# Turning tables and activation rows on TensorE instead of in DMAs, in a fused spectral filter and squared-ReLU kernel

## The chip, the core and the metric

The kernel runs on one core of a Trainium2 chip. The core has TensorE (PE, matrix products into PSUM), VectorE (DVE), ScalarE (ACT), GpSimd (POOL), SyncE (SP, which here issues every DMA) and 16 DMA engines. The metric is the device time of one execution in microseconds (us). All engines take their own instructions in order and wait for each other on semaphores.

## The reference

One token matrix of 2048 x 512 in bf16 goes through a spectral filter and then through a feed-forward layer (FFN), each behind a layer norm and each with a residual:

```python
def _A_ref(x, w_r, w_i):
    X = rfft2(x.astype(float32), axes=(-2, -1))
    X = X * (w_r + 1j * w_i)
    return irfft2(X, s=(S, D), axes=(-2, -1)).astype(bfloat16)

def _B_ref(x, w1, b1, w2, b2):
    h = einsum("bsd,df->bsf", x, w1) + b1
    r = where(h > 0, h, 0)
    return einsum("bsf,fd->bsd", r * r, w2) + b2

h  = x + _A_ref(_layernorm(x), A_w_r, A_w_i)
h2 = h + _B_ref(_layernorm(h), B_w1, B_b1, B_w2, B_b2)
```

D is 512, the FFN's inner width F is 1792.

## The kernel before

The tokens are laid out as 128 partitions by G = 16 groups (`xs`, token 16p + g), all in SBUF for the whole run. The two-dimensional Fourier transform and its inverse are done as matrix products with tables of cosines and sines that the kernel makes itself by integer ramps and ScalarE's sine. There are four stretches.

**Opening (about 0 to 18 us).** Loads of x; layer-norm statistics; the tables `KF`, `GF` and `EF`; the first product `p1` with `KR` (KF times the reciprocal deviation) into `Bt`.

**Middle (about 18 to 49.5 us).** For each of eight frequency blocks pr: the product `p2` (16 matmuls of 256 columns, for a pair of halves), its cast `U` on ACT, the product `p3` with `EF` (4 matmuls of 512 columns, or 12 for blocks 5 to 7), its cast `AB` on ACT, a butterfly `X` on DVE (blocks 1 to 4), the product `m` with the filter on DVE, two combinations `Z` and two folds `M` on DVE, the inverse product `p4` with `EI` on PE, its cast `T2` on ACT. Names such as p4-3-0 mean product p4, block 3, first half. At the end comes a short head for the first two token groups: `pd` (a product with `GI`), its cast `EO`, `yt`, the square `sq`, the sum `ss`, a logarithm and an exponential, and the normalised transposed rows `UT0`; beside it `py`, which with b2 gives the residual `hb`.

**FFN (about 49.5 to 154 us).** The 16 groups go in five chunks (2, 3, 4, 4 and 3 groups). Each chunk has 14 up products (`ph`/`sg` banks, L952), ReLU on ACT (L964), square on DVE (L970), and then the down products (`po`, L981). Between those, the next chunk is made ready: `p5`, `od`, `q`, `R`, `p6`, `hs` = x plus the filter's output, sum of squares on ACT (L757), reciprocal deviation on POOL (L896 to L900), the normalised rows `u` (L906 or L908), and their turned form `UT`, which the next chunk's up products read.

The transposed tables are made by DMA: `EI` from `EF` and `CN`, `KI` from `KF`, `GI` from `GF` (L454 to L465). So are `UT` of the groups in `TURN` = 2 and 5 to 15 (L801 and L921); groups 3 and 4 are turned by four 128 x 128 PE products into a `pp` bank (L932), which ACT or DVE copies to SBUF (L937). `GI`'s odd rows get a factor per partition from POOL (L495).

What sets the order: `Plan` takes every task with an estimated duration, reads, writes, a priority and a buffer, and hands out the order of each engine by its own clock of estimates. For the middle the order of PE, ACT and DVE is instead written out by hand (`MID`, L760), as is the start of the FFN (`DRAIN`, L995). The order of POOL and SP is always the planner's. Buffers matter: in the middle the large PSUM tiles `mm` are three, `U`, `m`, `X`, `Z` and `M` have two buffers each, `AB` three. `Z` of block 0 is read by p4-0 and so holds one of the two Z buffers until p4-0 is done.

Four lines that the prediction comes back to:

```python
EI = fwd.tile([P, 4, 9, P], BF16, name="EI")                 # L211
pool(0.5, lambda e=e: gp.tensor_scalar(GI[:, 1 + 2 * e], GI[:, 1 + 2 * e], hrow[:], 1.0, ALU.mult, ALU.mult), 410.0,  # L495
TURN = (2, *range(5, G))                                      # L801
pe.transpose(p[:, P * d:P * d + P], T["u", c][:, i, bass.ts(d, P)], ident[:])   # L932
```

Of the kernel before, what the change touches and what calls it, by code (L numbers as in the profile page):

```python
# [9 lines left out]
ALU = mybir.AluOpType  # L10
# [23 lines left out]
class Plan:  # L34
# [13 lines left out]
    def add(self, eng, w, fn, reads=(), writes=(), prio=0.0, alloc=None, at=0.0, shared=False, lag=0.0,  # L48
            uses=(), order=(), name=None):
        many = isinstance(eng, tuple)  # L50
        ways = dict(zip(eng, w)) if many else {eng: w}
        t = dict(many=many, eng=None, ways=ways, w=0.0, fn=fn, reads=list(reads), writes=list(writes), prio=prio, alloc=alloc, at=at,
                 shared=shared, lag=lag, end=None, order=list(order), n=len(self.tasks),
                 name=name or "-".join(map(str, writes[-1] if isinstance(writes[-1], tuple) else writes[-1:])))
        self.tasks.append(t)
        for k in t["writes"]:
            self.made.setdefault(k, []).append(t)
        for k in set(t["reads"]) | set(t["writes"]) | set(uses):
            self.use.setdefault(k, []).append(t)
# [85 lines left out]
def kernel(  # L145
# [52 lines left out]
    sq0 = persist.tile([P, 2, ND, P], BF16, name="sq0")  # L198
    rsb = persist.tile([P, 2, P], FP32, name="rsb")
    UT0 = persist.tile([P, 2, ND, P], BF16, name="UT0")  # L200
    EO = persist.tile([P, 2, 2, 256], BF16, name="EO")
    junk = persist.tile([P, D], BF16, name="junk")
    fz = persist.tile([P, 512], BF16, name="fz")
# [64 lines left out]
    def flat(t):  # L268
        n = len(t.shape)
        return t if n == 2 else t.rearrange("p a b -> p (a b)") if n == 3 else t.rearrange("p a b c -> p (a b c)")  # L270
# [180 lines left out]
            add(eng, ((0.37, 0.59), (0.42, 0.67))[t][n - 1], e2, reads=[k] + ["Btw"] * t, order=[("va", 4)] * t,  # L451
                writes=["Bt"] + ["BtD"] * (t == 1 and b == G), prio=56 + a)

    def tr_dma(i, dst, src, dep, prio):  # L454
        add("SP", 2.5, lambda: sy.dma_start(dst, src, transpose=True), reads=dep, order=[("EI", 2)] * (i == 3) + [("Wr", 1)] * (i < 2), writes=[("EI", i)], prio=prio, lag=(10.6, 10.4, 6.0, 6.0)[i])
    for i in range(2):
        tr_dma(i, EI[:, i], flat(EF[:, i]), [f"EF{i}"], 12 + i)
    tr_dma(3, KI[:], flat(KF[:]), ["KF"], 16)
    tr_dma(2, EI[:, 2], flat(EF[:, 2]), ["EF2"], 15)
    for pr in BY_Z:  # L460
        add("SP", 1.2, lambda pr=pr: sy.dma_start(EI[:, 3, pr], CN[:, pr - PE0], transpose=True), reads=["CN"],
            order=[("EI", 3)], writes=[("EI", 3, pr)], prio=17, lag=6.0)
    for t in range(2):
        add("SP", 1.3, lambda t=t: sy.dma_start(GI[:, :, P * t:P * t + P], flat(GF[:, t]), transpose=True), reads=[("gf", t)],
            order=[("EI", 3)], writes=[("gi", t)], prio=40.5 + t / 10, lag=12.0)  # L465
    for k, (d, s) in ((0, (W1[:], B_w1.rearrange("(c p) f -> p c f", p=P))),
                      (1, (W2[:], B_w2.rearrange("(i p) d -> p i d", p=P))),
                      (3, (b2b[:], B_b2.unsqueeze(0).to_broadcast([P, D])))):
        add("SP", 0.7, lambda d=d, s=s: sy.dma_start(d, s), writes=[("FW", k)], prio=40 + k, lag=15.0,
            order=[("gi", 1)] * (k > 0) + [("EI", i) for i in range(4)] + [("Wr", 0), ("Wr", 1), ("Wn", 0), ("Wn", 1)])  # L470

    PE0 = 5
    BY_PE = tuple(range(PE0, 8))
# [7 lines left out]
    def mid_tasks():  # L481
        def b1t():
            p = sg_tile(("b1",))
            mm(p[:, 0:NF], lhsT=b1b[:], rhs=ident[0:NF, 0:NF], start=True, stop=True)
            for g in range(2):
                mm(p[0:2, P + P * g:2 * P + P * g], lhsT=nmh[:, g], rhs=ident[:], start=True, stop=True)
        act(0.19, lambda: sc.copy(nmt[:], T[("b1",)][0:2, P:3 * P].rearrange("p (g c) -> p g c", g=2)), 142.0, reads=[("b1",)],
            writes=["nmt"], name="nmt")
        add("PE", 0.2, b1t, reads=["b1b", "ident", "nmh"], order=[("p3", 3)], writes=[("b1",)], prio=141.0, alloc=("sg", ("b1",)))
        act(0.19, lambda: sc.copy(b1f[:], T[("b1",)][:, 0:NF]), 142.0, reads=[("b1",)], writes=["b1f"])  # L490
        act(1.4, lambda: sc.preload_act_table_set("natural_log_exp_and_others"), 0.0, reads=["eps"], writes=["sqrt"])

        pool(0.2, lambda: gp.memset(ones[:], 1.0), 400.0, writes=["ones"])
        for e in range(2):
            pool(0.5, lambda e=e: gp.tensor_scalar(GI[:, 1 + 2 * e], GI[:, 1 + 2 * e], hrow[:], 1.0, ALU.mult, ALU.mult), 410.0,  # L495
                 reads=["hv", ("gi", 0), ("gi", 1)], writes=["GI"], name=f"GI-{e}")
        pool(0.15, lambda: gp.tensor_copy(nmh[:, :, 0], nm1[:, 0:2]), 401.0, reads=["nm1"], writes=["nmh0"])
        pool(0.15, lambda: gp.tensor_tensor(nmh[:, :, 1], nm1[:, 0:2], nmh[:, :, 0], ALU.subtract), 402.0, reads=["nmh0"],
             writes=["nmh"])
# [218 lines left out]
        for d in range(ND):  # L718
            mm(T["yt", g][:, P * d:P * d + P], lhsT=xs[:, g, P * d:P * d + P], rhs=ident[:], start=False, stop=False)
    for g in range(2):  # L720
        add("PE", 0.22, lambda g=g: cen(g), reads=["ones", "nmt"], order=[("p3", 7)], writes=[("yt", g, 0)],
            uses=[("yt", g)], name=f"yt-{g}-0", prio=170.0, alloc=("sg", ("yt", g)))
        add("PE", 0.22, lambda g=g: res(g), reads=["ident"], order=[("yt", g, 0)], uses=[("yt", g)],
            writes=[("yt", g, 1)], name=f"yt-{g}-1", prio=170.0)

    for g in range(2):
# [23 lines left out]
        def ut0(g=g):  # L750
# [2 lines left out]
        dve(0.66, ut0, -30.0, reads=[("r2", 0, g)], uses=[("yt", g)],   # L753
            writes=[("UT", 0), "UT0b" if g else "UT0a"], name=f"UT0-{g}")

    def sq_of(src, g):
        sc.activation(junk[:], src, ACT.Square, bias=nm1[:, g:g + 1], accum_out=ss2[:, g:g + 1])  # L757

    T["UT", 0] = UT0
    MID = {  # L760
        "PE": "p3-1 p2-2-0 p2-2-1 p2-4-0 p2-4-1 p2-3-0 p3-2 p2-3-1 p3-4 p2-6-0 p2-6-1 p3-3 p4-0-0 b1 "
             "p4-0-1 p3-6 p2-5-0 p2-5-1 p2-7-0 p2-7-1 p4-2-0 p4-2-1 p4-1-0 p4-1-1 p3-5 p3-7 p4-3-0 "
             "p4-3-1 p4-4-0 p4-4-1 p4-6-0 yt-0-0 p4-6-1 p4-5-0 yt-0-1 p4-5-1 p4-7-0a p4-7-1a p4-7-0b "
             "pd-0 pd-1 yt-1-0 yt-1-1 yt-0-2 yt-0-3 yt-1-2 yt-1-3 p4-7-1b ss-0 ss-1",
        "ACT": "AB-1 U-2 U-4 AB-2 U-3 AB-4 U-6 b1f AB-3 nmt T2-0 AB-6 U-5 U-7 T2-2 sqrt AB-5 T2-1 AB-7 "
              "T2-3 T2-4 T2-6 T2-5 T2a-7 EO-0 EO-1 sq-0 sq-1 sd-0-0 r2-0-0 sd-0-1 r2-0-1 T2b-7-1",
        "DVE": "m-0-0 m-0-1 Z-0-0 Z-0-1 X-1-0 X-1-1 m-1 Z-1-0 Z-1-1 M-1-0 X-2-0 X-2-1 M-1-1 m-2 X-4-0 "
              "Z-2-0 X-4-1 Z-2-1 m-4 M-2-0 Z-4-0 X-3-0 M-2-1 X-3-1 Z-4-1 m-3 M-4-0 Z-3-0 Z-3-1 m-6 "
              "M-4-1 M-3-0 Z-6-0 M-3-1 m-5 Z-6-1 Z-5-0 Z-5-1 m-7 M-5-0 M-5-1 Z-7-0 Z-7-1 M-7-0 M-7-1 "
              "T2b-7-0 UT0-0 UT0-1",  # L770
    }
    plan.run(MID)

# [24 lines left out]

    BY_PE2 = (2, 3, 4, 8)
    ONE = (1, 2, 3, 4)  # L800
    TURN = (2, *range(5, G))  # L801
    HBP = 0
    OWN = 1
    SPLIT = 2
# [2 lines left out]
    for c, (a, b) in enumerate(CHUNKS):  # L807
# [67 lines left out]
        if c == 0:  # L875
            for g in range(2):
                def d6(g=g, k=0):
                    py = (bank(("py", g), "po", 2) if k == 0 else T["py", g])[:]
                    if k == 0:
                        mm(py, lhsT=ident[:], rhs=xs[:, g, :], start=True, stop=False)  # L880
                    elif k == 1:
                        mm(py, lhsT=KI[:, 0], rhs=EO[:, g, 0].unsqueeze(1).to_broadcast([P, 2, 256]), start=False, stop=False)
                    else:
                        mm(py[:, 0:256], lhsT=KI[:, 0], rhs=EO[:, g, 1], start=False, stop=False)
                        mm(py[:, 256:512], lhsT=KI[:, 1], rhs=EO[:, g, 1], start=False, stop=True)
                for k in range(3):
                    add("PE", 0.22, lambda g=g, k=k, d6=d6: d6(g, k), reads=[["ident"], [("EO", g), ("EI", 3)], [("EO", g)]][k],
                        order=[("yt", 1, 3)] + [("py", g, j) for j in range(k)], uses=[("py", g)],
                        writes=[("py", g, k)] + [("py", g)] * (k == 2), name=f"py-{g}-{k}", prio=-3000.0 + g,
                        alloc=None if k else ("po", ("py", g)))  # L890
                dve(0.69, lambda g=g: ve.tensor_tensor(hb[:, g, :], T["py", g][:], b2b[:], ALU.add), -10.0,
                    reads=[("py", g), ("FW", 3)], order=[("UT", 0)] * OWN, writes=[("hb", g)])
        else:
            z = late + 50
            for k, (p0, p1) in enumerate([(g, g + 1) for g in range(a, b)] if c in ONE else [(a, b)]):
# [77 lines left out]
        for i in range(n):  # L973
            g = a + i
            for h in range(2) if g == G - 1 else (None,):
# [17 lines left out]
                add("SP", 0.1, lambda g=g, cs=cs: sy.dma_start(ov[:, g, cs], T["ot", g][:, cs]), reads=[("ot", g, h)],  # L993
                    writes=[("out", g)], uses=[("ot", g)], prio=nxt())
    DRAIN = {  # L995
        "PE": "py-1-0 py-0-0 py-1-1 py-0-1 py-1-2 py-0-2 pf-0 pf-1 p5-2 ph-0-0 ph-0-1 p5-3 ph-0-5 "
             "ph-0-3 ph-0-2",
        "ACT": "od-2 rl-0-0 rl-0-1 od-3 rl-0-5",
        "DVE": "hb-1 hb-0 q-2-0 q-2-1",
    }  # L1000
# [31 lines left out]
```

## Time and profile before

| what | value |
|---|---|
| time, median of 3 runs | 159.33 us (159.31 to 159.5) |
| time of the profiled execution | 158.99 us |
| its span in the profile | 157.2 us |
| granted TensorE clock | 1.00 in every stretch |
| DMA transposes | 12 of UT, 3 + 1 of EI, 1 of KI, 2 of GI |
| bytes moved by DMA | 14.02 MB |

The span is the profiler's own stretch from first to last record; 1.8 us of the execution lie outside it. "PE" is matmul, "PEld" the load of its stationary operand. A matmul's listed duration includes its way through the array, so matmuls overlap: what one costs PE is the distance to the next start, not its duration. Durations on DVE and ACT overlap a little in the same way.

### The profile page before, as it was taken

Reading aid. Unit: us, or ns where it says so; the run is one execution under the profiler, and the core shown is the slowest. Engines: PE = TensorE matmul, PEld = TensorE weight load, DVE = VectorE, ACT = ScalarE, POOL = GpSimd, SP = SyncE. Lnnn points to the kernel's source line nnn. Section 1 sums busy time; section 2 is a strip of 40 time slices with the busy share of each in tenths; the row PEclk is TensorE's granted clock in tenths of the full one; section 3 lists DMA queues with packets and bytes.
Section 4 is the critical chain, followed back from the end, with each engine's and each line's share of the span. In section 5 each row is a group of like instructions: output and inputs, shape, how many; then the busy total and the mean of one; then the engine's idle time right before and its main releaser. Section 6 shows DMA issues by size and latency. Waiting matters only on the chain.

```text
span 157.2 us, 2915 instructions
## 1 busy us (share of the span) xinstructions
PE 152.0 (97%) x1038; PEld 92.5 (59%) x1038; DVE 116.4 (74%) x310; ACT 102.0 (65%) x187; POOL 37.7 (24%) x84
## 2 busy tenths in 40 slices
PE   6998999999999999999999999999999999999992
PEld 4677876787788985556544544444544444555461
DVE  6999889999908987899832989981699963285221
ACT  8989689999767996599702889340688820288000
POOL 8898300005900024213400022530002340000000
PEclk9999999999999999999999999999999999999999
DMA  4957998799700001121121000324000412100011
GB/s 151 312 190 222 284 224 176 210 295 310 226 4 0 4 0 35 48 54 38 33 67 60 7 4 0 67 48 120 33 0 4 66 38 65 35 33 4 0 67 33
DMA packets 23449, 14.02 MB, mean 89 GB/s; under 512 B 12170, under 2 KB 22154, under 8 KB 23434
## 3 DMA queue, kind: packets, MB, share of 16 engines
q1 hardware_dynamic: 23434, 13.84, 33.5%
q8 instruction: 8, 0.13, 0.3%
q14 instruction: 7, 0.06, 0.1%
HBM read 8.92 MB, written 3.01 MB: 76 GB/s over the span
## 4 chain that ended last, share of the span: by engine, by line
PE 75%; DVE 14%; issue 3%; POOL 3%; DMA 2%; ACT 0%; DVEq 0%
PE po L981 31%; PE sg L952 20%; PE ph L952 11%; DVE Z L635 4%; DVE m L625 4%; DMA xs<-in_A_x_dram 2%; DVE X L611 2%; DVE st L395 2%; POOL KR L411 1%; PE pp L840 1%; DVE M L649 1%; DVE M L647 1%; POOL rs L402 1%; PE pp L847 1%; PE s_p L418 1%
## 5 line engine op out<-in xcount | busy, mean ns | idle before, releaser
L981 PE MATMUL po<-W,act 128*128 128x512 bf16 (+1 forms) x238 | 50.0, 367 | 0.0
L964 ACT ACTIVATE rl<-sg,b1f 128x512 bf16<-128x512 f32 (+2 forms) x46 | 27.4, 602 | 20.1 <-PE sg L952 19.1
L952 PEld LDWEIGHTS <-W 128*128 128x128 bf16 x288 | 26.9, 98 | 19.3
L952 PE MATMUL sg<-UT,W 128*128 128x512 bf16 (+3 forms) x188 | 37.6, 334 | 0.0
L981 PEld LDWEIGHTS <-act 128*128 128x128 bf16 x238 | 23.1, 98 | 24.3
L970 DVE TENSOR_TENSOR act<-rl 128x384 bf16<-128x384 bf16 (+2 forms) x70 | 25.2, 368 | 6.5 <-ACT rl L964 6.0
L990 DVE TENSOR_TENSOR ot<-po,hb 128x512 bf16<-128x512 f32 (+1 forms) x17 | 11.2, 660 | 22.0 <-PE po L981 21.9
L896 POOL TENSOR_SCALAR rs<-ss 128x1 f32<-128x1 f32 x14 | 5.8, 416 | 65.5 <-ACT junk L757 65.5
L952 PE MATMUL ph<-UT,W 128*128 128x384 bf16 (+3 forms) x100 | 20.5, 328 | 0.0
L964 ACT ACTIVATE rl<-ph,b1f 128x384 bf16<-128x384 f32 (+2 forms) x24 | 14.3, 596 | 8.2 <-PE ph L952 7.5
L757 ACT ACTIVATE junk<-hs,nm 128x512 bf16<-128x512 bf16 x14 | 10.0, 714 | 1.7 <-DVE hs L868 1.5
L868 DVE TENSOR_TENSOR hs<-pp,xs 128x512 bf16<-128x512 f32 x14 | 9.6, 689 | 1.8 <-PE pp L840 1.3
L495 POOL TENSOR_SCALAR GI<-GI,hrow 128x256 bf16<-128x256 bf16 x2 | 6.0, 2986 | 17.5 <-DMA GI<-GF 17.5
L506 PE MATMUL m_p<-U,EF 128*128 128x512 bf16 (+1 forms) x46 | 9.5, 337 | 0.0
L863 DVE TENSOR_TENSOR R<-q 128x127 bf16<-128x127 f32 x40 | 9.3, 285 | 0.0
L872 DVE TENSOR_TENSOR hb<-hs,b2b 128x512 f32<-128x512 bf16 x14 | 9.2, 684 | 0.0
L395 DVE BATCH_NORM_STATS2 st<-xs 128x6 f32<-128x512 bf16 x14 | 9.0, 672 | 0.1
L898 POOL TENSOR_TENSOR rs<-rs,mhalf 128x1 f32<-128x1 f32 x14 | 8.3, 596 | 1.2
L689 ACT CAST T<-m_p 128x1024 bf16<-128x1024 f32 (+1 forms) x8 | 7.5, 955 | 0.8 <-PE m_p L673 0.7
L908 ACT ACTIVATE u<-hs,nr,rs 128x512 bf16<-128x512 bf16 x5 | 4.1, 811 | 5.9 <-POOL nr L900 5.9
L246 PEld LDWEIGHTS <-fz 128*128 128x128 bf16 x69 | 5.5, 108 | 3.8 <-issue 1.6
L830 DVE TENSOR_TENSOR q<-pp,od 128x256 f32<-128x256 f32 x20 | 7.7, 417 | 0.0
(154 smaller groups left out, 230.4 us busy)
## 6 DMA issues: line engine op xcount, KB each, us to landing
W<-in_B_w_dram SPq DMA_DIRECT2D x2, 1792.0 KB, 8.5
out_dram<-ot SPq DMA_DIRECT2D x15, 128.0 KB, 1.8
xs<-in_A_x_dram SPq DMA_DIRECT2D x4, 256.0 KB, 3.6
xs<-in_A_x_dram SPq DMA_DIRECT2D x2, 512.0 KB, 6.1
W<-wx SPq DMA_DIRECT2D x2, 448.0 KB, 5.1
W<-in_A_w_r_dram SPq DMA_DIRECT2D x1, 512.0 KB, 8.6
W<-in_A_w_i_dram SPq DMA_DIRECT2D x1, 512.0 KB, 6.1
wx<-in_A_w_r_dram SPq DMA_DIRECT2D x1, 448.0 KB
```

What stands on the lines that cost most here:

```text
L395: ve.bn_stats(st[:], xs[:, g, :])
L506: mm(o.rearrange("p (j i e) -> p j i e", e=2, i=RUN), lhsT=w, rhs=U[:, q, s].rearrange("p (j e i) -> p j i e", e=2, i=RUN), **k)
L757: sc.activation(junk[:], src, ACT.Square, bias=nm1[:, g:g + 1], accum_out=ss2[:, g:g + 1])
L863: ve.tensor_tensor(o, x, y, (ALU.add, ALU.subtract, ALU.subtract, ALU.add)[k])
L868: dve(0.66, lambda g=g: ve.tensor_tensor(hs[:, g, :], T["p6", g][:], xs[:, g, :], ALU.add), z, reads=[("p6", g)], writes=[("hs", g)])
L872: add(("DVE", "POOL")[HBP], (0.62, 1.3)[HBP], lambda g=g: (ve, gp)[HBP].tensor_tensor(hb[:, g, :], hs[:, g, :], b2b[:], ALU.add), prio=lat ...
L898: pool(0.57, lambda p0=p0, p1=p1: gp.tensor_tensor(rs2[:, p0:p1], rs2[:, p0:p1], mhalf[:, 0:p1 - p0], ALU.pow), z, reads=[("sd", c, k)], w ...
L952: mm(p[:, P * i0:P * i1], lhsT=W1[:, d, bass.ts(f, P)], rhs=T["UT", c][:, i0:i1, d, :], start=(d == 0), stop=(d == ND - 1))
L964: sc.activation(r[:, 0:P * n], T["ph", c, f][:, 0:P * n], ACT.Relu, bias=b1f[:, f:f + 1], scale=1.0)
L970: ve.tensor_tensor(t[:, f, 0:P * n], r[:, 0:P * n], r[:, 0:P * n], ALU.mult)
L981: mm(p[:, cs], lhsT=T["act", c][:, f, bass.ts(i, P)], rhs=W2[:, f, cs], start=(f == 0), stop=(f == NF - 1))
L990: ve.tensor_tensor(o[:, cs], T["po", g, h][:, cs], hb[:, g, cs], ALU.add)
```

## The change

- `TURN` becomes empty: the rows of all 14 groups after the first two are turned by four PE products and a copy on ACT or DVE.
- The tables are turned by PE in the middle: four tasks `tS`, `tC`, `tK`, `tG` with 8, 8, 4 and 8 products with the identity, each into an `mm` tile. ACT casts them to SBUF: `EI-0`, `EI-1` (128 x 1024), `EI-z`, `EI-k` (128 x 256), `GI-0`, `GI-1` (128 x 512, the second with the factor per partition, which takes the two POOL steps of L495 away).
- `EI`'s third table, the negative of its first (128 x 1152), is made by POOL (`EI-n`), and so is one block of the fourth (`EI-n6` in the text, block 6). Every p4 reads the third table's key.
- The x of the first two groups is added to b2 by DVE ahead of time (`xb`, into a new tile `hb0`), and the two PE products of `py` that added x are gone.
- The loads of W1, b2 and W2 are issued right after the filter's loads, in that order.
- `MID` and `DRAIN` are new orders; the start of `yt-1` now waits in the planner for p4-7's first half.

```diff
+    hb0 = persist.tile([P, 2, D], FP32, name="hb0")
...
-    for i in range(2):
-        tr_dma(i, EI[:, i], flat(EF[:, i]), [f"EF{i}"], 12 + i)
-    tr_dma(3, KI[:], flat(KF[:]), ["KF"], 16)
-    tr_dma(2, EI[:, 2], flat(EF[:, 2]), ["EF2"], 15)
...
-        for e in range(2):
-            pool(0.5, lambda e=e: gp.tensor_scalar(GI[:, 1 + 2 * e], GI[:, 1 + 2 * e], hrow[:], 1.0, ALU.mult, ALU.mult), 410.0,
-                 reads=["hv", ("gi", 0), ("gi", 1)], writes=["GI"], name=f"GI-{e}")
+        def turned(name, blocks, reads, order=()):
+            def go():
+                p = mm_tile((name,))
+                for j, x in enumerate(blocks):
+                    mm(p[:, P * j:P * j + P], lhsT=x, rhs=ident[:], start=True, stop=True)
+            add("PE", 0.062 * len(blocks), go, reads=["ident", *reads], order=order, writes=[(name,)], name=name, prio=79.0, alloc=("mm", (name,)))
...
+        turned("tS", [EF[:, 0, k, :] for k in range(1, 9)], ["EF0"])
+        turned("tC", [EF[:, 1, k, :] for k in range(1, 9)], ["EF1"])
+        turned("tK", [EF[:, 0, 0, :], EF[:, 1, 0, :], KF[:, 0], KF[:, 1]], ["EF0", "EF1", "KF"])
+        turned("tG", [GF[:].rearrange("p t r c -> p t (r c)")[:, t, P * j:P * j + P] for j in range(4) for t in range(2)], [("gf", 0), ("gf", 1)])
+        for i in range(2):
+            act(0.97, lambda i=i: sc.copy(flat(EI[:, i, 1:9]), T[("tS", "tC")[i],][:]), 79.5, reads=[(("tS", "tC")[i],)], writes=[("EI", i)], name=f"EI-{i}")
+        act(0.35, lambda: sc.copy(EI[:, 0:2, 0, :], T["tK",][:, 0:256].rearrange("p (i c) -> p i c", c=P)), 79.6, reads=[("tK",)], writes=[("EI", 0), ("EI", 1)], name="EI-z")
+        act(0.35, lambda: sc.copy(flat(KI[:]), T["tK",][:, 256:512]), 120.0, reads=[("tK",)], writes=[("EI", 3)], name="EI-k")
+        pool(3.0, lambda: gp.tensor_scalar(EI[:, 2], EI[:, 0], -1.0, None, ALU.mult), 80.0, reads=[("EI", 0)], writes=[("EI", 2)], name="EI-n")
+        for pr in BY_Z:
+            pool(0.4, lambda pr=pr: gp.tensor_scalar(EI[:, 3, pr], EI[:, 1, pr], -1.0, None, ALU.mult), 100.0, reads=[("EI", 1)], writes=[("EI", 3, pr)], name=f"EI-n{pr}")
+
+        def gi(j):
+            sc.activation(GI[:, j::2], T["tG",][:].rearrange("p (j c) -> p j c", c=256)[:, j::2], ACT.Identity, scale=hrow[:] if j else 1.0)
+        for j in range(2):
+            act(0.57, lambda j=j: gi(j), 140.0, reads=[("tG",), "hv"], writes=["GI"], name=f"GI-{j}")
...
+    for g in range(2):
+        dve(0.62, lambda g=g: ve.tensor_tensor(hb0[:, g, :], xs[:, g, :], b2b[:], ALU.add), 420.0 + g,
+            reads=[("x", g), ("FW", 3)], order=[("M", 7)], writes=[("xb", g)])
...
+        "PE": "tK p2-4-0 p2-4-1 p3-1 p2-3-0 p2-3-1 p3-4 p2-5-0 p2-5-1 p3-3 p2-2-0 b1 p2-2-1 tS p3-5 "
+             "p3-2 tC p2-7-0 p2-7-1 p2-6-0 p2-6-1 p4-0-0 p4-0-1 p4-1-0 p4-1-1 p4-4-0 p4-4-1 p3-6 "
+             "p4-3-0 p4-3-1 p3-7 p4-5-0 p4-5-1 tG p4-2-0 p4-2-1 p4-6-0 p4-6-1 yt-0-0 p4-7-0a p4-7-1a "
+             "p4-7-0b p4-7-1b pd-0 yt-1-0 pd-1 yt-0-1 yt-0-2 yt-0-3 yt-1-1 yt-1-2 yt-1-3 ss-0 ss-1",
+        "ACT": "EI-z EI-k U-4 AB-1 U-3 AB-4 U-5 AB-3 U-2 EI-0 AB-5 AB-2 EI-1 U-7 U-6 T2-0 T2-1 T2-4 sqrt "
+              "AB-6 T2-3 AB-7 T2-5 GI-0 b1f nmt GI-1 T2-2 T2-6 T2a-7 T2b-7-0 EO-0 EO-1 sq-0 sq-1 sd-0-0 "
+              "r2-0-0 sd-0-1 r2-0-1",
+        "DVE": "m-0-0 m-0-1 Z-0-0 Z-0-1 X-1-0 X-1-1 m-1 X-4-0 X-4-1 m-4 X-3-0 Z-4-0 Z-4-1 X-3-1 M-4-0 "
+              "M-4-1 m-3 Z-1-0 Z-1-1 X-2-0 M-1-0 M-1-1 X-2-1 m-5 Z-3-0 Z-5-0 Z-5-1 Z-3-1 M-5-0 M-3-0 "
+              "M-3-1 m-2 Z-2-0 M-5-1 Z-2-1 M-2-0 m-6 M-2-1 Z-6-0 m-7 Z-6-1 Z-7-0 Z-7-1 M-7-0 M-7-1 "
+              "T2b-7-1 xb-0 xb-1 UT0-0 UT0-1",
...
-    TURN = (2, *range(5, G))
+    TURN = ()
...
-                    if k == 0:
-                        mm(py, lhsT=ident[:], rhs=xs[:, g, :], start=True, stop=False)
...
+                dve(0.69, lambda g=g: ve.tensor_tensor(hb[:, g, :], T["py", g][:], hb0[:, g, :], ALU.add), -10.0,
+                    reads=[("py", g), ("xb", g)], order=[("UT", 0)] * OWN, writes=[("hb", g)])
```

## The prediction

> **What bounds the kernel now.** I read the page's busy rows first, then the windows by stage, then the chain of waits, then the timelines of PE, DVE and POOL.
>
> ```profile
> PE 152.0 (97%) x1038; PEld 92.5 (59%) x1038; DVE 116.4 (74%) x310; ACT 102.0 (65%) x187; POOL 37.7 (24%) x84
> PE   6998999999999999999999999999999999999992
> ```
>
> An average of 97% does not say that PE is at its peak, so next comes one table by stage: the middle up to DVE's last fold, the short head, the FFN. Its columns are the window, its length, the busy time of PE, PEld, DVE, ACT and POOL, then clock, DMA share and GB/s.
>
> ```profile
> 20.85:43.20 22.35, 22.20 (x182) 16.44 (x179) 21.71 (x46) 20.62 (x25) 5.96 (x2) 1.00 0.97 239
> 43.20:49.50 6.30, 6.18 (x64) 4.73 (x65) 2.01 (x4) 4.87 (x11) 0.00 (x0) 1.00 0.01 3
> 49.50:154.20 104.70, 104.70 (x637) 57.15 (x635) 73.51 (x200) 58.89 (x123) 16.86 (x42) 1.00 0.14 35
> ```
>
> In the FFN PE has no idle time. It is dense in truth: the chain of waits has 37 down products in 7.99 us, 0.216 us each for 512 columns, at a clock of 1.00. In the middle three engines are full at once: idle in those 22.35 us are PE 0.15, DVE 0.64, ACT 1.73. No compute wait there is for a transposing DMA; the only long wait on one is POOL's 17.5 us for GI, and GI was ready (42.93) before pd read it (44.47). So what the change removes costs nothing now, and what it adds falls on engines without slack.
>
> **FFN rows.** The price of a turn stands in the trace, since groups 3 and 4 are turned by PE already:
>
> ```profile
> 58.16 3.19 PE L981 MATMUL po<-W,act 128*128 128x512 bf16 x14
> 61.18 0.39 PE L932 MATMUL pp<-ident,u 128*128 128x128 bf16 x4
> 61.41 1.24 PE L981 MATMUL po<-W,act 128*128 128x512 bf16 x5
> ```
>
> Start to start a group costs 0.23 us (61.18 to 61.41), though its four matmuls have 0.39 us listed; by the chain it is 0.22. Twelve more groups are 12 x 0.22 = +2.64 us. The Trainium skill ("VectorE: DVE Perf Modes", The three transpose paths) recommends TensorE for a 128x128 transpose where PSUM is acceptable, and gives 390 ns for one against 1309 by DMA. By that price the 48 turns are 18.7 us; pipelined, the row decides. And the rule compares latencies: the DMA's latency was hidden, PE's time is not.
>
> Twelve evictions come too (0.577 us on ACT, L937): 6.9 us. In the down phases ACT and DVE are nearly empty (105 to 110 us: ACT 0.00, DVE 1.29 of 5), so most hide. Two per chunk fall into the end of an up phase (95 to 100: ACT 4.82, DVE 4.67 of 5), where three banks and PE's 0.864 us per f against ACT's 0.68 leave some room. New, too, is that PE itself waits for u: behind a late turn all down products queue, where before only SP's queue did. POOL's chain before u took 0.19 + 0.55 + 0.19 us mostly, but once 1.94 us for the first step. Below: 0 (the existing two turns had no wait). Above: one such lateness in about one group of twelve plus 0.5 us of full ACT in each of three chunks, 3 us. I take +0.3, nearer to the two turns seen.
>
> **Middle, by sums.** PE: 28 turned blocks at 0.057 (the row above) = 1.6, less 0.15 idle. ACT: EI-0 and EI-1 at 0.91 (two T2 casts take 1.93, one 1.02, so a following one adds 0.91), EI-z and EI-k at 0.27 (od to the next start, 50.35 to 50.62), GI twice 0.48 (EO: 1.07 for two, 0.59 for one): 3.3, less 1.73 idle = +1.6. The swap of the two T2b halves lies behind T2a.
>
> **Middle, walked through.** I put these durations into the new orders. PE: 0.87 per p2 and p4, 0.865 or 1.73 per p3; PE to ACT 0.2; DVE: 0.34 for X, Z, M and 1.14 for m. PE starts at 20.85 with tK and is dense; ACT takes EI-z at 21.58, EI-k 21.85, U-4 22.14, AB-1 23.05 (end 24.06, before 22.92), U-3 23.96, AB-4 24.87, U-5 25.78, AB-3 26.69, U-2 27.65, EI-0 28.56 (end 29.58), AB-5 29.82, AB-2 30.73 (end 31.75), EI-1 31.64, U-7 32.55, U-6 33.46, T2-0 34.37. PE reaches p4-0 at 32.67. DVE: X-1 24.08, m-1 24.87, X-4 26.01, m-4 26.80, X-3 27.94, m-3 29.96, Z-1 31.10, X-2-0 at 31.77, m-5 33.1, Z-3-0 34.25, Z-5-0 about 34.6. From m-4's start to X-2-0 DVE has no gap.
>
> **The negation on POOL.** EI-n can start at 29.7, and p4-0 wants it at 32.67. Nearest rows: KR (before the middle), GI (in it), and 1152 elements of int32 in the opening.
>
> ```profile
> L411 POOL TENSOR_SCALAR KR<-KF,rs x8: 478/480/481, 7.2 to 12.8; 128x256 bf16<-128x256 bf16 x8
> L495 POOL TENSOR_SCALAR GI<-GI,hrow x2: 883/2986/5090, 37.0 to 42.0; 128x256 bf16<-128x256 bf16 x2
> L353 POOL TENSOR_SCALAR fiE<-idxE,cE x1: 1232/1232/1232, 4.8 to 4.8; 128x1152 int32<-128x1152 int32 x1
> ```
>
> The same 256 elements took 0.48 us in the opening and 5.09 in the middle. Where that instruction ended is seen in DVE:
>
> ```profile
> 40.95 0.42 DVE L647 TENSOR_TENSOR M<-Z 128x512 bf16<-128x512 bf16 x1
> 41.29 0.41 DVE L649 TENSOR_TENSOR M<-Z 128x512 bf16<-128x512 bf16 x1
> 41.74 0.92 DVE L635 TENSOR_TENSOR Z<-m 128x512 bf16<-128x512 bf16 x2
> ```
>
> POOL ran from 36.96 to 42.05. DVE's instructions overlapped without a break up to 41.70; 0.04 us of gap was enough, and the next two Z took 0.92 in place of 0.76: now DVE was held. The rule behind it is the Trainium skill's ("SBUF — State Buffer", Who interferes with whom): a DVE instruction with two SBUF inputs and a GpSimd instruction that reads SBUF exclude each other, for the whole instruction. That speaks against this change: it puts 1152 elements there, into the same kind of stretch. By the row of the opening EI-n is 1.23 and ends at 30.9, hidden; by row and rule it waits for DVE's first gap and then holds DVE about 1.0 us.
>
> When is that gap? X-2-0 needs AB-2, which ends at 31.75, against DVE's 31.77: a tie; any hop more on the ACT side opens it. Taking it: EI-n 31.8 to 32.95, p4-0 at 33.0, still ahead of T2-0's turn on ACT (34.37). DVE goes on 1.1 us later. From there ACT leads: T2-1 35.28, T2-4 36.19, table load 37.10, AB-6 38.38, T2-3 39.29, AB-7 40.45, T2-5 41.36, GI-0 42.27, GI-1 43.05, T2-2 43.53, T2-6 44.85, T2a 45.76, pd-0 46.1. Before, pd-0 began at 44.47: **+1.65**, as the sums say. EI-n6 waits behind EI-n for another gap and is wanted only at about 43, after such gaps.
>
> **Edits with one answer.** Head after pd: two py products of 0.217 us leave PE, but UT0-0 ended at 49.12 and pf began at 49.48, so 0.25 is gained. xb (2 x 0.68) lies in DVE's 3.9 us of waiting before T2b; without that cover UT0 would be 1.4 later. The POOL GI steps free nothing. The weight loads move ahead of 18.3 to 24.8 on SP, where the EI transposes stood: W<-wx is issued before them and landed in about 5.1, so by 23.3; m-1 needs it at 24.87. W1 is needed at 49.5. Nothing.
>
> **Sum.** 1.65 - 0.25 + 2.64 + 0.3 = +4.3 on the span of 157.2, so 161.5; with the 1.8 outside it 163.3 for the profiled run of 158.99, and **163.7** against the median of 159.33.
>
> **Rivals.** *Starved longer*: X-2-0 comes without a gap. DVE then runs on to Z-5-0 at 34.6. Z has two buffers, Z of block 0 holds one until p4-0, so Z-5-0 stands until p4-0 is done: EI-n 34.67 to 35.8, p4-0 to 36.75. The ACT list then starts T2-0 at 36.95 instead of 34.37, pd-0 comes at about 48.3, +3.85: **165.9**. For it: GI's 5.09. Against: a gap of hundredths suffices.
>
> *PE stalls in the FFN*: the upper bound of 3 us in place of 0.3 on the turns: **166.4**. For it: 1.94 us on POOL and ACT at 4.82 of 5; against: no such wait at the two turns seen.
>
> *Faster*: the turns slip into PE's holes. The old middle was shaped by tables arriving by DMA (first use of EI at 27.86); PE's holes and fillers between 17.8 and 49.5 are about 1.5 us (7 filler products at 17.65, 7 at 44.08, 3 at 47.50, a few of 0.2). If the new order closes all of them, 1.6 of turned tables cost 0.1, py's 0.43 is won, and if the FFN's turns hide in the overlap of neighbouring matmuls as well, the time is **159.0**. It decides only where a turn of the FFN costs PE under 0.03 us; the 0.22 from start to start speaks against it, and so does DVE, which has no such holes.
>
> *Turns or middle partly hidden*, holes taken up: 1 us less of each, **161.7**.
>
> **Numbers.** Forecast 0.45, starved 0.30, FFN stalls 0.13, partly hidden 0.08, faster 0.04. The range goes from 162.2 (forecast without stall and with part of the middle hidden) to 167.2 (starved, plus 1.3 us of FFN stalls), leaving out 2 in 10. A change of 0.2% (0.3 us) is about what can be told from none: faster 0.03, same 0.02, slower 0.95.
>
> **What would show it.** Right: PE without idle time in the FFN and 14 groups at L932, 0.22 each; pd-0 near 46.1; EI-n on POOL well over 1.23 us, ending just after a gap in DVE, with a DVE instruction stretched there. Wrong: FFN length unchanged at 104.7 us, EI-n at 1.2 us beside a full DVE, or pf before 49.5. If p4-0 starts after 35 the starved case holds.

## The result, and the profile after

The changed kernel takes **167.44 us** (median of 4 runs, 167.19 to 167.62) against 159.32 before: a ratio of 1.0508, 95% interval 1.049 to 1.0527. The direction was as forecast, the size was not: +8.1 us in place of +4.3, and 0.24 us above the end of the range.

The profiled execution took 167.19 us with a span of 165.4. Its page, with the busy row, PE's row in 40 slices of 4.1 us, and one group of the list of the costliest:

```profile
PE 155.8 (94%) x1106; PEld 96.2 (58%) x1115; DVE 122.2 (74%) x317; ACT 109.0 (66%) x200; POOL 37.8 (23%) x84
...
PE   7979999959998999999999999989999999999992
...
L498 POOL TENSOR_SCALAR EI<-EI 128x1152 bf16<-128x1152 bf16 x1 | 5.1, 5097 | 10.4 <-ACT EI L495 10.4
```

PE worked 3.8 us longer than before and its share still fell from 97% to 94%: it now waits as well. The 5 in its row, the ninth slice, is at 33 to 37 us in the middle; the later of the two single 8s is at 107 to 112 us in the FFN. The windows by stage, with the same columns as in the prediction, from the first turned table to `pd`, from `pd` to the first up product, and the FFN:

```profile
21.08:48.55 27.47, 25.22 (x229) 19.07 (x227) 24.78 (x46) 24.96 (x33) 5.86 (x2) 1.00 0.46 153
48.55:53.74 5.19, 4.67 (x49) 3.51 (x47) 2.97 (x5) 4.01 (x9) 0.00 (x0) 1.00 0.00 0
53.74:162.40 108.66, 107.28 (x677) 59.63 (x683) 75.50 (x206) 62.36 (x130) 16.97 (x42) 1.00 0.06 20
```

Where both kernels have the same markers (the first `p2` product, the first `pd`, the first up product, the end), the 8.2 us of span split like this:

| stretch | before | after | change | forecast |
|---|---|---|---|---|
| opening, to the first p2 | 18.04 | 18.27 | +0.23 | 0 |
| middle, to pd | 26.43 | 30.28 | +3.85 | +1.65 |
| head, pd to the first up product | 5.01 | 5.19 | +0.18 | -0.25 |
| FFN, from there to the end | 107.72 | 111.66 | +3.94 | +2.94 |

The change leaves the compute of the opening as it was, and its first p2 starts anywhere from 18.04 to 19.42 us in the profiles of this study; 0.23 is within that scatter. So from here on stretches are compared, not only times.

**In the middle** the negation is the place. Rows from the timelines of the changed kernel, POOL, then DVE, then PE:

```profile
30.07 5.10 POOL L498 TENSOR_SCALAR EI<-EI 128x1152 bf16<-128x1152 bf16 x1 [10.41 <-ACT EI L495]
...
31.39 0.75 DVE L644 TENSOR_TENSOR Z<-m 128x512 bf16<-128x512 bf16 x2
32.14 3.06 DVE L620 TENSOR_TENSOR X<-AB 128x512 bf16<-128x512 bf16 x1
...
35.22 0.22 PE L678 MATMUL m_p<-EI,Z 128*128 128x128 bf16 x1 [1.92 <-DVE X L620]
```

POOL has its input at 30.07 and waits while DVE runs without a break. At 32.14, at X-2-0, it gets in: a DVE instruction that takes 0.42 elsewhere takes 3.06. What such an instruction takes over its usual 0.42 is called the hold below: here 2.64 us. PE does the one p4-0 product that needs no third table (33.08) and stands until 35.22. The name that the profile gives as PE's releaser, DVE's X, is the instruction that ended beside POOL's, not the cause: p4-0 reads `EI`, which POOL wrote.

**In the FFN** PE had no idle time before and has 1.38 us now. The longest wait stands before a turn. From the timelines of POOL, DVE and PE:

```profile
105.55 1.94 POOL L908 TENSOR_SCALAR rs<-ss 128x1 f32<-128x1 f32 x1 [2.58 <-ACT junk L770]
...
106.15 1.28 DVE L886 TENSOR_TENSOR hb<-hs,b2b 128x512 f32<-128x512 bf16 x2
...
107.36 1.24 PE L993 MATMUL po<-W,act 128*128 128x512 bf16 x5
109.29 0.40 PE L944 MATMUL pp<-ident,u 128*128 128x128 bf16 x4 [0.69 <-ACT u L920]
```

Five down products are issued in 1.08 us, so PE was done at 108.44 and stood for 0.85. The chain behind it: POOL's 128 x 1 step, mostly 0.19 us, ended only when DVE's two hb did (two SBUF inputs each), then the power, then u on ACT, then the turn. Before the change the same step took 1.94 us too, as its row there shows; the turn was a DMA then, and PE waited for nothing in the FFN:

```profile
99.90 1.94 POOL L896 TENSOR_SCALAR rs<-ss 128x1 f32<-128x1 f32 x1 [2.59 <-ACT junk L757]
```

### The profile page after: what moved, and what is told of

Read it like the earlier page. It is cut to its first block, busy times and chain, and to the rows that moved or that the text cites. A ratio compares the mean times of both kernels' runs of the same rounds, so it can differ in the third digit from the quotient of the medians.

```text
span 165.4 us, 3028 instructions
## 1 busy us (share of the span) xinstructions
PE 155.8 (94%) x1106; PEld 96.2 (58%) x1115; DVE 122.2 (74%) x317; ACT 109.0 (66%) x200; POOL 37.8 (23%) x84
## 4 chain that ended last, share of the span: by engine, by line
PE 68%; DVE 15%; POOL 7%; ACT 5%; issue 3%; ACTq 0%; POOLq 0%; DVEq 0%
PE po L993 25%; PE sg L964 18%; PE ph L964 9%; DVE m L634 5%; DVE X L620 3%; DVE Z L644 2%; PE pp L944 2%; POOL rs L908 2%; PE m_p L536 2%; DVE st L396 1%; ACT junk L770 1%; POOL KR L412 1%; ACT u L920 1%; POOL rs L403 1%; ACT rl L976 1%
## 5 line engine op out<-in xcount | busy, mean ns | idle before, releaser
L920 ACT ACTIVATE u<-hs,nr,rs 128x512 bf16<-128x512 bf16 x7 | 5.7, 816 | 4.6 <-POOL nr L912 4.6
L498 POOL TENSOR_SCALAR EI<-EI 128x1152 bf16<-128x1152 bf16 x1 | 5.1, 5097 | 10.4 <-ACT EI L495 10.4
```

## Experiments

Fourteen kernels were run. "Before" was run beside each of them, at 159.3 to 159.5.

**The two halves of the change, apart and together.** First the negation on DVE:

```diff
-        pool(3.0, lambda: gp.tensor_scalar(EI[:, 2], EI[:, 0], -1.0, None, ALU.mult), 80.0, ...
+        dve(0.45, lambda: ve.tensor_scalar(EI[:, 2], EI[:, 0], -1.0, None, ALU.mult), 80.0, ...
-              "M-4-1 m-3 Z-1-0 Z-1-1 X-2-0 ...
+              "M-4-1 m-3 EI-n Z-1-0 Z-1-1 X-2-0 ...
```

> The changed kernel with the negation EI-n (128 x 1152) moved from POOL to DVE, right after m-3 in DVE's order; all else as changed. Theory A (the POOL negation holds DVE's port for about 3 us, and p4-0 with all behind it waits): the 3.06 us at X-2-0 go, p4-0 runs through from 33.1, T2-0 starts near 34.6 in place of 36.25, the middle is 1.7 to 2.2 us shorter: 165.2 to 165.8. Theory B (the middle is longer because ACT and PE carry turned tables and casts, and the negation hides behind them): 167.0 to 167.5.

Measured: 165.54 (ratio 1.0384, 1.0345 to 1.0423). The negation took 0.45 us, X-2-0 took 0.42 again, PE did not wait at p4-0, and the middle measured 27.94 from p2 to pd: 2.34 less than in the changed kernel, and 1.51 more than before. The time gains less, 1.9; in the profiled run the opening was 0.75 longer. Theory A holds. The second POOL step, 128 x 128, now came to stand in DVE's dense stretch. X-2-0, then POOL's timeline, then DVE's:

```profile
33.17 0.42 DVE L620 TENSOR_TENSOR X<-AB 128x512 bf16<-128x512 bf16 x1
...
33.86 5.78 POOL L500 TENSOR_SCALAR EI<-EI 128x128 bf16<-128x128 bf16 x1 [13.45 <-ACT EI L495]
...
38.00 1.22 DVE L634 TENSOR_TENSOR m<-X,W 128x2048 bf16<-128x2048 bf16 x1
39.25 0.43 DVE L644 TENSOR_TENSOR Z<-m 128x512 bf16<-128x512 bf16 x1
```

It was locked out for over five microseconds, up to the first break in DVE, 0.03 us at 39.22, where Z needs the m just before it. Nobody needed its result yet.

Then the FFN's rows by DMA again, in the changed kernel (`TURN = (2, *range(5, G))`), and the converse, `TURN = ()` in the kernel before:

> The changed kernel with TURN as before (12 groups turned by DMA again). If the FFN's growth of 3.94 us is the turns and the waits of PE behind them: FFN back to about 104.7 us and 163.5. If only the PE time of the turns comes back (12 x 0.22 = 2.64) and the waits have another cause: 164.8. If PE's turns were hidden and something else made the FFN longer: 167.4.

> The kernel before with TURN empty, nothing else: the FFN part of the change alone. Turns and waits: 159.3 + 3.9 = 163.2. Turns without waits (the planner finds slots where u is ready, as for groups 3 and 4): 162.0. Hidden: 159.3.

Measured: 163.95 (1.0280, 1.0232 to 1.0328) and 163.39 (1.0252, 1.0229 to 1.0276). In the profiles the FFN took 107.7 us with the DMAs and 111.35 with the turns in the old kernel, against 107.72 and 111.66. So the turns cost 3.6 to 4.0 us, of which 12 x 0.22 = 2.64 is PE's work and the rest, 1.0 to 1.3, is waiting. (163.95 is a median that lies between two runs at about 163.3 and two at about 164.6, in which PE's clock was lower; the last section has them.)

> Both: negation on DVE and TURN as before. What is left is the middle's added PE and ACT work and the head. If the parts add up: 167.4 - 1.9 - 3.9 = 161.6, that is 2.3 over the kernel before. If the new middle without the POOL hold were as good as the old one: 159.3 to 159.6.

Measured: 161.14 (1.0108, 1.0086 to 1.0130). The parts add up: 1.7 us over before are left, and its stretches say where: middle +1.52, head +0.18, FFN 0.00. The +1.52 is the new middle without the POOL hold. It agrees with the +1.6 that the forecast's sums gave for the turned tables and their casts; but the written orders changed with them, and no run takes the two apart.

**What the negation costs on POOL.** A first attempt at a price added a negation to the kernel before, for DVE's idle stretch:

```diff
+        pool(3.0, lambda: gp.tensor_scalar(scr[:], EI[:, 0], -1.0, None, ALU.mult), 500.0, reads=[("EI", 0), "T2a"], writes=["scr"], name="scr")
```

> The kernel before with one more POOL instruction whose result nothing reads: the negation of EI's first table (128 x 1152 bf16) into a scratch tile, due after T2a, in DVE's idle stretch of about 44 to 47. It prices the negation with nothing in its way. Theory A (POOL's own work on 1152 bf16 elements is about 3 us, so the 3.06 us at X-2-0 were the whole instruction): 2.2 (KR's 0.48 per 256 elements, scaled) to 3.1. Theory B (about 1.2 us as in the int32 row, stretched to 3 by taking turns with DVE): 1.1 to 1.4. Time unchanged, 159.3.

Measured: 164.85, a single run, and not what was meant. The read of T2a binds the planner alone, so POOL began at 43.40, ahead of DVE's last fold, and held it: that fold took 3.14 us in place of 0.41, and PE, which waits for it, stood for 2.8. As a price it serves all the same, as POOL's row and DVE's show:

```profile
43.40 3.32 POOL L498 TENSOR_SCALAR scr<-EI 128x1152 bf16<-128x1152 bf16 x1
...
43.62 3.14 DVE L651 TENSOR_TENSOR M<-Z 128x512 bf16<-128x512 bf16 x1
```

One DVE instruction with 0.41 us of work was not through until POOL was, so the two did not take turns, and POOL's own time for this step is about 3 us. Theory A.

Why three microseconds, when 1152 elements of int32 took 1.23? The int32 step has two operations and a value per partition, as have KR and GI; the negation has one operation with a constant, and nine rows of 128. The changed kernel was run with EI-n in their form, and then with one difference at a time:

```diff
-gp.tensor_scalar(EI[:, 2], EI[:, 0], -1.0, None, ALU.mult)
+gp.tensor_scalar(flat(EI[:, 2]), flat(EI[:, 0]), mone[:], 1.0, ALU.mult, ALU.mult)
...
+gp.tensor_scalar(flat(EI[:, 2]), flat(EI[:, 0]), -1.0, None, ALU.mult)
...
+gp.tensor_scalar(EI[:, 2], EI[:, 0], -1.0, 1.0, ALU.mult, ALU.mult)
```

> The changed kernel with EI-n in the form of KR and GI (two multiplications, the first by a value per partition, on a flat row of 1152). If the 3 us are POOL's price for 1152 bf16 elements in any form: hold on DVE about 3 us, 167.4. If they come from the form with one constant and a two-level row: 2.2 us or less by KR's 0.48 per 256, p4-0 earlier by 0.9, 166.5.

> The changed kernel with EI-n as one multiplication by a constant, as changed, but on a flat row of 1152 in place of 9 rows of 128. If the pattern of the operands sets POOL's price: the hold at X-2-0 falls to about 1.0 us, 165.8. If the single operation or the constant sets it: 2.7, 167.4.

> The changed kernel with EI-n as two multiplications by constants (-1 and 1) on 9 rows of 128. If the single operation is the slow form: hold about 1.0 us, 165.8. If the row pattern or the constant operand is: 2.7, 167.4.

Measured: 165.79 (1.0395, 1.0366 to 1.0424), 167.97 (two runs, 167.42 and 168.53), 166.32 (two runs, 165.84 and 166.81). X-2-0 took 1.37, 3.07 and 1.28 us. The rows, in DVE's timeline of the run with a flat row and of the one with two operations:

```profile
32.20 3.07 DVE L620 TENSOR_TENSOR X<-AB 128x512 bf16<-128x512 bf16 x1
```

```profile
32.57 1.28 DVE L620 TENSOR_TENSOR X<-AB 128x512 bf16<-128x512 bf16 x1
```

Less its own 0.42, the hold is 0.95, 2.65 and 0.86 us. It is the single operation: with a second multiplication, by 1, the hold is a third. The rows make no difference with one operation (2.64 against 2.65); with two, rows and constant together make 0.09. The middle took 28.6 and 28.5 us with two operations. Why POOL does so stays open.

**The waits in the FFN.** Two groups back to DMA, first 8 and 12 (`TURN = (8, 12)`), which turned out to be the wrong ones:

> The changed kernel with groups 8 and 12 alone turned by DMA: the two at which PE stood waiting for u. If PE's waits behind late turns are a cost of their own: 2 x 0.22 + about 1.3 = 1.7 less, 165.7. If the waits only move to other groups or other engines: 0.44 less, 167.0.

Measured: 166.91 (1.0476, 1.0444 to 1.0507), FFN 111.20: 0.46 less, two turns' work and no more. In this trace the waits still stand, before the turns of groups 7 and 11: they had been put down to the wrong groups. A miss as a test, but a clean price of 0.23 per turn. Then `TURN = (7, 11)`:

> The changed kernel with groups 7 and 11 turned by DMA. The trace of the run with 8 and 12 shows that PE's two waits (0.5 and 0.85 us) stand before the turns of groups 7 and 11, so that run had left them in place. If the waits are PE held in order behind a late u: 2 x 0.22 + 1.3 = 1.7 less, 165.7. If they move on to 8 and 12: 0.44 less, 167.0.

Measured: 166.76 (1.0444, 1.0408 to 1.0480; 165.87 to 167.43). The FFN took 110.36, that is 1.30 less: 0.44 of work and 0.86 of waiting. Part of the wait stayed (0.7 us by PE's loads), now before group 8 in the same down phase. The median shows less of it: the profiled run and one more had a lower clock (mean 0.99; last section), and its middle is 1.0 longer for it. The two runs at 1.00 took 165.87 and 166.41, that is 1.0 to 1.6 less than the changed kernel.

The order can be mended without giving back a turn: a higher estimate for the POOL step moves the turns back in PE's queue.

```diff
-                pool(0.15, lambda p0=p0, p1=p1: gp.tensor_scalar(rs2[:, p0:p1], ss2[:, p0:p1], 1.0 / D, EPS, ALU.mult, ALU.add),
+                pool(1.4, lambda p0=p0, p1=p1: gp.tensor_scalar(rs2[:, p0:p1], ss2[:, p0:p1], 1.0 / D, EPS, ALU.mult, ALU.add),
```

> The changed kernel with the planner's estimate for the first step to the reciprocal deviation at 1.4 us in place of 0.15, so that it puts the turns later in PE's order; no instruction is added or taken away. Waits behind a late u: 1.0 to 1.3 less, 166.2. If the turns then come too late for the next chunk's up products, or nothing waits for u: 167.4 or more.

Measured: 166.69 (1.0452, 1.0423 to 1.0480), FFN 110.59: 1.07 less with the same instructions, and no wait for u among PE's waits. So the waits were the place of the turns in an in-order queue, not the evictions; 2.88 over the run with rows by DMA are left, 0.24 per turn. The step moved to ACT instead:

```diff
-                pool(0.15, lambda p0=p0, p1=p1: gp.tensor_scalar(rs2[:, p0:p1], ss2[:, p0:p1], 1.0 / D, EPS, ALU.mult, ALU.add),
+                act(0.2, lambda p0=p0, p1=p1: sc.activation(rs2[:, p0:p1], ss2[:, p0:p1], ACT.Identity, scale=1.0 / D, bias=eps[:]),
```

> The changed kernel with the first of the three steps to the reciprocal deviation (a 128 x 1 multiply-add, POOL before) on ACT, right behind the sum of squares. In the changed kernel that step took 1.94 us once, beside DVE's hb with two SBUF inputs, and PE then waited 0.85 us at group 12. If DVE's hold on POOL is the cause of the wait: 0.5 to 1.0 less, 166.5 to 166.9. If ACT's load or the order is: 167.3 to 167.8.

Measured: 168.86 (1.0593, 1.0558 to 1.0629). A miss: in its profile the opening was 1.15 us late and the middle 0.98 longer at a lower clock, which says nothing of the edit; but its one run at a clock of 1.00 took 168.29, and the FFN is 0.38 longer as well. PE waits for ACT's eviction of a turned group then (0.56 us). POOL's lock-out can be told from this run only so far: taking the step off POOL does not help when it goes on the engine that also evicts.

**A version that beats both?** The one part with a forecast gain is xb:

> The kernel before with xb alone: x plus b2 on DVE ahead of time, the two py products of x gone, everything else and every other order as before. If the prediction's term holds: 0.25 less, 159.1. If the head is set by the chain of square, logarithm and UT0 and not by PE: no change, 159.3 to 159.5. If xb holds UT0 up: 160 or more.

Measured: 159.40 (14 runs; ratio 0.9996, 0.9983 to 1.0008): no change. The two products are gone, and PE waits instead, on the first up product of its timeline:

```profile
49.02 0.27 PE L888 MATMUL po<-EO,KI 128*128 128x256 bf16 x1
49.63 0.38 PE L955 MATMUL ph<-UT,W 128*128 128x128 bf16 x4 [0.33 <-ACT T L690]
```

This product reads nothing that ACT's T2b-7-1 writes, so what it waits for is the PSUM bank from which ACT copies T2b-7-1, last in ACT's list. With both halves of T2b moved ahead of the head, as the change has them:

> The kernel before with xb (as run before alone) and the two T2b halves ahead of the head: p4-7-1b before pd, T2b-7-0 on ACT right after T2a, T2b-7-1 on DVE right after the last fold. With xb alone PE had its 0.43 us back but pf then waited 0.33 us for ACT's T2b-7-1. Theory (that wait ate the gain): pf follows UT0-0 at once, 0.25 less than before, 159.2. Rival (the filler products ahead of pd were cover, p4-7-1b now delays pd): 159.5 to 159.9.

Measured: 159.81 (22 runs; 1.0021, 1.0010 to 1.0031), the head 5.10 in place of 5.01. The rival was right: the middle is 0.17 longer with p4-7-1b ahead of pd, and in the head py now stands 0.57 before its first product, until ACT's second logarithm has read its bank. That is a little more than the wait that went. Nothing tried beats the kernel before.

## Where the prediction was right, and where it failed

- **What bounds it**: right. PE is full in the FFN, three engines are in the middle, and the removed DMAs had cost nothing; with rows by DMA and the negation on DVE the kernel is still 1.1% slower than before.
- **Turns in the FFN, 12 x 0.22**: right; 0.23 per turn measured by taking two away. **Stalls, +0.3**: wrong, 1.3. Both ends of the bound were named, and so was the 1.94 us step; the value was taken near the two turns seen in the old trace, which did not wait. Of twelve more two met a u that was 0.5 and 0.85 us late. Two rows were too few to stand for twelve.
- **Middle by sums**: right, +1.6 against 1.5 without the hold. **By the walk**: the order of events was right (X-2-0 met at a tie, p4-0 wanted at 32.9 with this run's opening, first product issued at 33.08), the end was not. It has +1.65 with a hold of 1.0; with a hold of 0.86 the middle measured +2.08.
- **The step that failed: "it waits for DVE's first gap and then holds DVE about 1.0 us".** The place and the lock until POOL is through are as foretold. The duration was taken from the int32 row, an instruction with two operations, as the KR and GI rows beside it are. With two operations the hold is 0.86 to 0.95, as written; with the one operation that the change uses it is 2.64. p4-0 thus came at 35.2 in place of 33.0, past T2-0's turn on ACT at 34.37, and the rest of the middle followed. With two operations the middle took 28.5 us in place of 30.28, so the size of this one term is 1.8 of the 3.9 us of span missed; the others are the walk's 0.4, the FFN's waits 1.0, the head 0.4 and the opening 0.2.
- **A second step, "From there ACT leads"**: a hold of 0.86 was free for T2-0 (35.13 in the run with two operations, 0.1 behind the walk when the openings are set equal), but not for what follows. DVE's last stretch of Z begins 0.68 later there than in the run with the negation on DVE (44.08 and 43.73, openings set equal), and PE waits for it before the second half of p4-6:

```profile
44.56 1.05 PE L682 MATMUL m_p<-EI,Z 128*128 128x256 bf16 x8 [0.24 <-DVE Z L644]
```

  With the negation on DVE it does not wait there, and the middle is 0.6 shorter (27.94).
- **Head, -0.25**: wrong, +0.18. The new order puts yt-1's start between the two pd, so the second EO comes 0.86 after the first where it came 0.48 after it, and py, which before had been issued during the logarithms, waits for one; it reads no logarithm, so the wait is for its PSUM bank. No run takes the two causes apart. From PE's timeline before, then from that of the changed kernel:

```profile
48.12 0.59 PE L880 MATMUL po<-xs,ident 128*128 128x512 bf16 x2
...
52.02 0.38 PE L752 MATMUL m_ss<-sq,ones 128*128 128x128 bf16 x4
52.87 0.59 PE L894 MATMUL po<-EO,KI 128*128 128x512 bf16 x2 [0.47 <-ACT rsb L754]
```

  The saved products were replaced by a wait, in this order and, by the run with xb alone, in the old one. "Leaves PE" is not "leaves the path" where PE's next instruction needs a bank that ACT frees.
- **Rivals**: "starved longer" did not come: POOL got in at X-2-0, not at Z-5-0. That the middle's +3.85 is exactly that case's number is chance. Its sign, p4-0 after 35, was met (35.22) and misleads, since a long hold delays p4-0 as much as a late start does. "PE stalls in the FFN" came in part, 1.3 of its 3, beside the hold and not in its place. The range's upper end did add a starved middle and 1.3 us of stalls, 167.2; head and opening, 0.7 over the forecast together, were allowed for in no case and put the time past it.

## What to carry to other kernels

A DMA whose latency was hidden cost nothing here; to replace it by work on a full engine costs that work, and in an in-order queue also every lateness of its input that the DMA's own queue had absorbed. A GpSimd elementwise step beside a dense run of two-input VectorE instructions has two prices, the wait for a break and the time for which it then locks VectorE out, so price it by a row with the same number of operations, or put it on VectorE, where this one took 0.45 us. When a wait moves, look at what the next instruction of that engine needs besides the data: twice here a PSUM bank took back what two removed products had given.

## What the runs showed of the hardware

**A second operation made this GpSimd step shorter.** 1152 bf16 elements times -1 held DVE 2.64 and 2.65 us as a single multiplication, 0.86 and 0.95 as two.

**A break of hundredths of a microsecond decides.** Before the change POOL waited 4.7 us for GI (36.96 to 41.70), and with the negation on DVE 5.4 us for 128 x 128 (33.86 to 39.22), each time up to a break of 0.03 to 0.04 us between two DVE instructions. In the changed kernel DVE's rows only touch at 32.14, where the others overlap by 0.07 to 0.09, and that was enough.

**A stand of two to three microseconds can halve PE's clock for the next three to six.** In the windows of the run with the negation added to the old kernel (columns as before, the clock third from the end) PE stood from 44.0 to 46.8, and its clock then was 0.50 for 5.7 us:

```profile
44.00:46.80 2.80, 0.02 (x1) 0.00 (x0) 2.76 (x1) 0.60 (x1) 2.72 (x1) 0.82 0.03 6
46.80:52.50 5.70, 5.68 (x35) 3.92 (x36) 0.00 (x0) 1.67 (x4) 0.00 (x0) 0.50 0.00 0
```

In the run with a flat row PE stood 2.1 us at p4-0 and then had 0.57 for 4 us (0.50 in the two full microseconds from 37 to 39):

```profile
33.00:36.00 3.00, 1.07 (x17) 0.91 (x15) 3.00 (x4) 1.92 (x3) 2.99 (x2) 1.00 0.14 45
36.00:40.00 4.00, 4.00 (x24) 2.69 (x22) 3.53 (x10) 2.38 (x3) 0.00 (x0) 0.57 0.00 0
```

The changed kernel's own profile has the same stand with a clock of 1.00 behind it, so at two microseconds it falls either way. The runs' mean clocks say how often. Of the 26 runs of the seven kernels that kept the stand at p4-0, 10 have a mean clock of 0.988 to 0.990: none of the changed kernel's four, two of four with the FFN's rows by DMA, three of four with the step on ACT. With rows by DMA these two took 164.48 and 164.80 us, the two at 1.00 took 163.16 and 163.43. In the kernels without such a stand, before included, no run is under 0.997. What decides was not tried.
